# Two more units by 32x32 squares in an attention and feed-forward kernel, with their loads on GpSimd's queue and single rooms refilled behind each transpose

## The chip, the cores and the metric

The kernel runs on one core of a Trainium2 chip. A core has five engines with a queue of instructions each: TensorE (PE in the profile, its weight loads PEld), VectorE (DVE), ScalarE (ACT), GpSimd (POOL) and SyncE (SP), which here only issues transfers. The metric is the time of one execution on the device in microseconds (us).

## What is computed

Two blocks, one after the other. The first is a gated linear recurrence over 768 tokens for each of 4 batches and 8 heads, with 48 values a head. Its output, 3072 rows of 384, goes through a SwiGLU feed-forward block with 1536 hidden values. The three weight matrices arrive as 64-bit floats and are converted on the chip.

```python
f = 1.0 / (1.0 + np.exp(-f_logit))
for t in range(S):
    state = f[:, :, t, :, None] * state + np.einsum('bhd,bhe->bhde', k[:, :, t], v[:, :, t])
    y[:, :, t] = np.einsum('bhd,bhde->bhe', q[:, :, t], state)
...
x = np.ascontiguousarray(attn_out.transpose(0, 2, 1, 3)).reshape(B * S, H * D)
g = x @ w_gate
silu = g * (1.0 / (1.0 + np.exp(-g)))
val = x @ w_val
return (silu * val @ w_out).astype(np.float32)
```

## The kernel before

The work runs in `short_path`. The 768 tokens are cut into six chunks of 128. One *unit* of attention is one batch of one chunk, so units 0 to 3 are chunk 0, units 4 to 7 chunk 1, and so on to unit 23. A chunk that has gone through attention goes through the feed-forward block while the next chunk's attention is threaded between its matmuls. Chunk 0 uses plain products (`mlp_plain`, lines 790 and 813); chunks 1 to 5 use a scheme with fewer products (`mlp_fifteen`, line 992, and `down_seven`, lines 1091 and 1154), which needs sums of weights and of tokens on VectorE (lines 893 and 896).

`attention(u)` is a generator of 15 steps. In order: the gate's sigmoid and its transpose; the transpose of k; a running product of the gates backwards (line 605, `tail`, with a reciprocal at 608); k times tail (`kT`, line 559); for most later units a write of kT to memory, to be read back turned (lines 620 to 623 and 662); a running sum of products forwards (line 631, `gate`); the transpose of q; q times gate (`qT`, line 559, then a memset of one column of the gates by GpSimd at line 639); the scores on TensorE (line 651); their mask on VectorE (line 666); the decayed state; the output y (lines 687 to 727); and the new state (lines 732 to 741). The smallest product of a unit is kept in `least` (line 629 or 658), which at the end decides whether a general path has to redo everything.

The inputs lie token by token, and the attention wants them value by value, so f, k and q have to be transposed. There are two ways:

- Chunks 0 and 1 (`c < SQUARES`, `SQUARES = 2`): each input is loaded whole into a `raw` tile (line 444, on SyncE's queue), and TensorE transposes it in four blocks of 128x128 into PSUM (`transposed`, line 579), where ScalarE applies the sigmoid (line 590) and VectorE reads k and q in its multiplies. There are two raw tiles for each of f, k and q, used in turn. The rows are padded from 48 to 64 values; the padding of f holds 60, that of k and q holds 0 (line 343).
- Chunks 2 to 5: four transfers for each input (line 440, SyncE's queue) lay it into a `room` in a form whose 32x32 squares VectorE can transpose at once (line 593 for f, after a sigmoid in place at 584; line 601 for k; line 635 for q). `kp` is then the unit's qT tile and `qp` its tail tile, as rooms to transpose into. There is one room for each of f, k and q. They are made by `make_rooms` once the tiles of the early part are given up.

`load(u, what)` issues a unit's loads; `load_after(u)` issues those of a later one: for units 4 and 5 the loads of the unit two later, right after qT, and from chunk 2 on f, q and k of the next unit, all together after the transpose of q at line 635. The values v have tiles of their own.

What sets the order: the beginning, to line 1259, and everything from line 1286 on run in the order written, engine by engine (`in_order`). The latter part is written by a plan: a list of due times in units of a product's length (`times`, `CHAINS`, `SCORES`). Between the two, where units 4 to 7 are threaded through the plain feed-forward block (`attention_steps`, `take_turns`), each engine's order is chosen when the program is built, by what a model of the machine finds ready and by the order written. `attention_steps` cuts the 15 steps of a unit into four pieces of 3, 6, 3 and 3 and interleaves the pieces of neighbouring units. Conversions of weights (line 478 to 491) and weight sums are threaded through the same stretch; `behind` ties sums behind the last VectorE instruction written.

[...] a transfer on SyncE's queue that waits for a room holds all transfers behind it.

Of the kernel before, what the change touches and what calls it, by code (L numbers as in the profile page):

```python
# [9 lines left out]
FP32 = mybir.dt.float32  # L10
# [280 lines left out]
def short_path(ctx, tc, ident, least, judge, q, k, v, f_logit, moe_w_gate, moe_w_val, moe_w_out, out):  # L291
# [9 lines left out]
    nc = tc.nc  # L301
    B, H, S, D = q.shape
    C = 128
    NCH = S // C
    HP = H // 2
    W = 64
# [6 lines left out]
    NRAW = 2  # L313
    NROT = 2
    NV = 4
    SQUARES = 2
# [9 lines left out]
    first_pool = early.enter_context(tc.tile_pool(name="first", bufs=1))  # L326
# [9 lines left out]
                            pattern=[[1, C]], channel_multiplier=-1)  # L336


    raw = {nm: [first_pool.tile([128, H, W], FP32, tag=f"{nm}raw{i}", name=f"{nm}raw{i}") for i in range(NRAW)]
           for nm in "qkf"}  # L340
    for nm in "fkq":
        for t in raw[nm]:
            nc.gpsimd.memset(t[:, :, D:W], 60.0 if nm == "f" else 0.0)
# [20 lines left out]
    def pairs(t, off=0):  # L364
        return t[:, off:off + HP * N1].rearrange("p (a t) -> p a t", t=N1)
# [23 lines left out]
    units = [(b, c) for c in range(NCH) for b in range(B)]  # L389
# [5 lines left out]
    Q = 32  # L395
    NI = C // Q
    RUN = NI * D

    rooms = {}

    def make_rooms(pool):
        for nm in "fkq":
# [3 lines left out]
    def v_of(u):  # L406
        return vs[u % (NV if units[u][1] < SQUARES else NV // 2)]

    def squares(nm):
        return rooms[nm][:, Q:Q + HP * RUN].rearrange("t (a i e) -> t a i e", a=HP, i=NI)[:, :, :, 0:Q]  # L410

    def split_squares(nm):
        return squares(nm).rearrange("t a (j i) e -> t a j i e", j=2)

    def in_turn(t):

        return t.rearrange("p a (t i) -> p a i t", i=NI)

    def parted(t):

        return t.rearrange("p (j a t i) -> p a j i t", j=2, a=HP, i=NI // 2)

    def load(u, what="fkqv"):
        b, c = units[u]
        rows = slice(c * C, (c + 1) * C)
        inputs = dict(f=f_logit, k=k, q=q, v=v)
        for nm in "fkqv" if c < SQUARES else "fqkv":
            src = inputs[nm]  # L430
            if nm not in what:
                continue
            if nm == "v":
                dst = v_of(u)
            elif c < SQUARES:
                dst = raw[nm][u % NRAW]
            else:
                for n in range(4):
                    at = Q * (1 - n % 2)
                    nc.sync.dma_start(  # L440
                        out=rooms[nm][Q * n:Q * (n + 1), at:at + HP * RUN].rearrange("t (a e) -> t a e", a=HP),
                        in_=src[b, n // 2::2, rows, :].rearrange("a (t i) d -> t a (i d)", i=NI))
                continue
            nc.sync.dma_start(out=dst[:, :, 0:D], in_=src[b, :, rows, :].rearrange("h t d -> t h d"))

# [87 lines left out]
    def bank(name):  # L533
        return banks[-1].tile([128, 512], FP32, tag="a", name=name)
# [10 lines left out]
    def attention(u):  # L545
        b, c = units[u]
# [2 lines left out]
        gate, tail = (x[u % NROT if c < SQUARES else 0] for x in (gates, tails))  # L549

        diagonal = None

        def multiply(out, x, by):

            if c >= SQUARES:
                for_each = "p a (t j i) -> p a t j i"
                out, by = (t.rearrange(for_each, j=2, i=NI // 2) for t in (out, by))
                x = x.rearrange("p (j a t i) -> p a t j i", j=2, a=HP, i=NI // 2)
            nc.vector.tensor_tensor(out, x, by, ALU.mult)  # L559
# [16 lines left out]
        def transposed(name, src):  # L576
            p = bank(name)
            for a in range(HP):
                nc.tensor.transpose(p[:, a * C:(a + 1) * C],
                                    src[:, 2 * a:2 * a + 2, :].rearrange("t r d -> t (r d)"), ident)  # L580
            return p.rearrange("p (a t) -> p a t", t=C)

        if c >= SQUARES:
            nc.scalar.activation(squares("f"), squares("f"), AF.Sigmoid)
            if b == (c > SQUARES):

                nc.scalar.activation(spare, spare, AF.Silu)
        else:
            p = transposed("fTp", fr)
            nc.scalar.activation(pairs(gate)[:, :, 1:N1], p, AF.Copy if u in ahead else AF.Sigmoid)  # L590
        yield
        if c >= SQUARES:
            nc.vector.transpose(in_turn(pairs(gate)[:, :, 1:N1]), squares("f"))
        yield

        kT = att.tile([128, HP, C], FP32, tag="kT", name="kT")
        qT = att.tile([128, HP, C], FP32, tag="qT", name="qT", bufs=2)
        kp, qp = kT, qT
        if c >= SQUARES:
            kp = qT.rearrange("p a t -> p (a t)")  # L600
            nc.vector.transpose(parted(kp), split_squares("k"))
        yield

        n = HP * N1
# [2 lines left out]
        whole = pairs(tail)[:, :, 1:2]  # L607
        nc.vector.reciprocal(pairs(start)[:, :, 0:1], whole)
        yield
        if c < SQUARES:  # L610
            kp = transposed("kTp", kr)
            qp = transposed("qTp", qr)
        multiply(kT, kp, pairs(tail, 2)[:, :, 0:C])
        yield
        turned = SQUARES < c < NCH - 1
        if turned:


            beside = rooms["k"][:, 0:HP * C].rearrange("p (i m) -> p i m", i=NI)
            nc.vector.transpose(beside.rearrange("p i (a e) -> p a i e", e=Q), kT.rearrange("p a (i e) -> p a i e", e=Q))  # L620
            turn = turn_pool.tile([Q, NI, HP, NI, Q], FP32, tag="turn", name="turn")
            for r in range(NI):
                nc.sync.dma_start(out=turn[:, :, :, r, :].rearrange("t i a e -> t (i a) e"),
                                  in_=beside[Q * r:Q * (r + 1)].rearrange("t i (a e) -> t (i a) e", e=Q))
        yield

        if c >= SQUARES:

            nc.scalar.copy(least[:, u, :], whole.rearrange("p a t -> p (a t)"))
            whole = least[:, u, :].unsqueeze(2)  # L630
        nc.vector.tensor_tensor_scan(gate[:, 0:n], gate[:, 0:n], start, 1.0, op0=ALU.mult, op1=ALU.add)
        yield
        if c >= SQUARES:
            qp = tail[:, 0:HP * C]
            nc.vector.transpose(parted(qp), split_squares("q"))
            load_after(u)
        yield
        multiply(qT, qp, pairs(gate)[:, :, 1:N1])
        nc.gpsimd.memset(pairs(gate)[:, :, 0:1], 0.0)  # L639
        if 0 < c < SQUARES:  # L640
            load_after(u)
        if c < SQUARES:
            decay()
        yield
# [7 lines left out]
        if c < NCH - 1 and not turned:  # L652
            p = bank("kt")
            for a in range(HP):
                nc.tensor.transpose(p[:, a * C:(a + 1) * C], kT[:, a, :], ident)
        yield
        if c < SQUARES:
            nc.scalar.copy(least[:, u, :], whole.rearrange("p a t -> p (a t)"))
        if c < NCH - 1:
            kt = att.tile([128, HP * C], FP32, tag="kt", name="kt")  # L660
# [14 lines left out]
        if c and b < B - 1:  # L675
# [20 lines left out]
            for h in range(H):  # L696
                a, par = h // 2, h % 2
                f = h * D
                while f < (h + 1) * D:
                    n = min((h + 1) * D, (f // 128 + 1) * 128) - f  # L700
# [4 lines left out]
        else:  # L705
# [15 lines left out]
            for par in range(2):  # L721
                for n in range(DM // Q):
                    h = n // per * 2 + par
# [5 lines left out]
        if c < NCH - 1:  # L729
            p = bank("dS")  # L730
# [4 lines left out]
        if c >= SQUARES and u + 2 < len(units):  # L735
            load(u + 2, "v")
# [4 lines left out]
            nc.vector.tensor_tensor(states[b], decayed[:, :, 0:D], dS, ALU.add)  # L741
        yield

    def load_after(u):

        w = u + (1 if units[u][1] >= SQUARES else 2)
        if w < len(units) and (units[w][1] >= SQUARES) == (w == u + 1):
            load(w, "fkqv" if units[w][1] < SQUARES or w == SQUARES * B else "fkq")

    def attention_steps(c):  # L750

        runs = [attention(c * B + b) for b in range(B)]
        parts = [3, 6, 3, 3]
        order = sorted((2 * b + s, b, n) for b in range(B) for s, n in enumerate(parts))
        return [lambda b=b, n=n: [next(runs[b]) for _ in range(n)] for _, b, n in order]

    traced = nc.cur_bb.bb.instructions

    def in_order(since, engines):

# [6 lines left out]
    def keep_order(mine):  # L767
        for a, b in zip(mine, mine[1:]):
            tc.add_manual_dep(b, a.name, mybir.DependencyInfo(mybir.DependencyClass.NoSync,
                                                              mybir.DependencyReason.DATA), reason="order")  # L770
# [427 lines left out]
    for u in range(NRAW):  # L1198
        load(u, "fkq")
    load(0, "v")  # L1200
    mark = traced[-1]
    keep_warm(5)
    first = [attention(b) for b in range(B)]
    done = [0] * B

# [37 lines left out]

    hidden, last = mlp_plain(0)
    steps = attention_steps(1)
    sigmoid_ahead(B)
    joins.pop(0)()
# [41 lines left out]
    for c in range(2, NCH):  # L1289
        for b in range(B):  # L1290
            run = attention(c * B + b)
            waiting += [((c - 2) * whole + t, lambda run=run: next(run)) for t in times(c)[b]]
# [33 lines left out]
def kernel(  # L1326
# [22 lines left out]
    def judge(bank):  # L1349
# [13 lines left out]
        yield  # L1363

    short_path(tc, ident, least, judge, *args)
    with tc.If(redo[0] > 0, label="redo"):
        general_path(tc, *args)
# [32 lines left out]
```

## Time and profile before

| | us |
|---|---|
| median of 3 runs (607.35 to 608.85) | 607.47 |
| the profiled execution, its own time | 607.02 |
| its span, first to last instruction | 605.3 |

The stages of the profiled execution, from its timeline: attention of chunk 0 to 29.6; plain feed-forward of chunk 0 with attention of chunk 1 to 144.1; then the five chunks of the scheme with fewer products, to 600. The table shows the busy time of the engines in stretches, in us.

| stretch | length | TensorE | VectorE | ScalarE | GpSimd |
|---|---|---|---|---|---|
| 0 to 30 | 30 | 24.04 | 26.30 | 12.45 | 3.16 |
| 30 to 145 | 115 | 114.73 | 95.40 | 56.27 | 1.00 |
| 145 to 240 | 95 | 94.06 | 83.03 | 48.52 | 15.64 |
| 240 to 264 | 24 | 23.24 | 21.40 | 13.66 | 3.27 |
| 264 to 596 | 332 | 332.00 | 248.13 | 161.55 | 47.30 |

The clock granted to TensorE is full through all of it (0.998 in the mean). A matmul's recorded length overlaps that of the next, so what a group of matmuls holds the engine for is read from the start of one group to the start of the next.

### The profile page before, as it was taken

What the parts mean: (1) busy time and instruction counts of PE and PEld (TensorE: products, weight loads), DVE (VectorE), ACT (ScalarE), POOL (GpSimd) and SP (SyncE); (2) the same over time, 40 slices, a digit from 0 to 9 for tenths busy, and PEclk for the clock granted to TensorE, in tenths of its full rate; (3) what the DMA queues carried; (4) which work ended last, traced back from release to release, by engine and by line L of the source; (5) the groups of instructions that cost most, each with busy time, mean ns of one, the idle gap of its engine ahead of it and who ended that gap; (6) DMA issues with size and microseconds to landing.
All of it is one profiled execution on the core that took longest, in us unless ns stands there. A gap on an engine that the chain in (4) does not pass through costs nothing.

```text
span 605.3 us, 10815 instructions
## 1 busy us (share of the span) xinstructions
PE 592.4 (98%) x4028; PEld 487.7 (81%) x4028; DVE 476.5 (79%) x825; ACT 292.5 (48%) x557; POOL 70.4 (12%) x175
## 2 busy tenths in 40 slices
PE   7899999999999999999999999999999999999996
PEld 5744545667888899878899988899988899988896
DVE  7999895968999977989995978995878982566741
ACT  3567662314876521476632376742276740366600
POOL 1000000000030050030330030330030321000000
PEclk9999999999999999999999999999999999999999
DMA  9999371014231144443345243244231100100001
GB/s 198 242 251 357 136 198 27 7 27 138 80 82 48 45 117 104 104 112 96 73 112 127 78 117 95 53 120 110 74 105 52 28 7 9 53 1 1 1 1 56
DMA packets 110299, 55.11 MB, mean 91 GB/s; under 512 B 72992, under 2 KB 102688, under 8 KB 110240
## 3 DMA queue, kind: packets, MB, share of 16 engines
q1 hardware_dynamic: 103872, 47.67, 30.0%
q0 software_dynamic: 4352, 3.94, 1.9%
q10 hardware_dynamic: 2016, 2.75, 1.2%
q8 instruction: 33, 0.54, 0.4%
q14 instruction: 26, 0.21, 0.1%
HBM read 44.56 MB, written 6.82 MB: 85 GB/s over the span
## 4 chain that ended last, share of the span: by engine, by line
PE 87%; DVE 9%; issue 1%; ACT 1%; DMA 1%; SPq 0%; DVEq 0%; ACTq 0%
PE o L1091 19%; PE A L992 15%; PE B L992 12%; PE gate L790 5%; PE val L790 5%; PE c L992 5%; PE o L992 5%; PE sc L651 4%; PE o L1154 3%; PE o L813 3%; PE y L691 2%; PE y L712 2%; PE dS L732 2%; PE y L687 1%; DVE c L896 1%
## 5 line engine op out<-in xcount | busy, mean ns | idle before, releaser
L702 POOL DMA_DIRECT2D xT<-yT x120 | 60.1, 509 | 54.2 <-ACT yT L695 51.7
L992 PE MATMUL A<-xs,w_both 128*128 128x256 f32 x240 | 62.3, 382 | 0.8 <-ACT c L997 0.8
L1091 PE MATMUL o<-w_out,h 128*128 128x192 f32 x360 | 62.0, 327 | 0.5 <-DVE h L944 0.5
L1091 PEld LDWEIGHTS o<-w_out,h 128*128 128x128 f32 x360 | 58.7, 190 | 1.7 <-DVE h L944 0.8
L997 ACT COPY c<-A 128x512 f32<-128x512 f32 x40 | 23.3, 584 | 57.7 <-PE A L992 57.7
L997 ACT COPY aside<-A 128x512 f32<-128x512 f32 x60 | 35.1, 585 | 33.1 <-PE A L992 33.0
L992 PEld LDWEIGHTS A<-xs,w_both 128*128 128x128 f32 x240 | 44.8, 190 | 7.7 <-ACT c L997 1.2
L893 DVE TENSOR_TENSOR c<-c,aside 128x512 f32<-128x512 f32 x60 | 41.1, 685 | 12.4 <-ACT aside L997 10.8
L944 DVE TENSOR_TENSOR h<-h,c 128x256 f32<-128x256 f32 x100 | 40.5, 413 | 7.8 <-ACT h L1008 7.6
L666 DVE TENSOR_TENSOR A<-sc,causal 128x512 f32<-128x512 f32 x48 | 30.9, 684 | 17.6 <-PE sc L651 17.6
L1008 ACT ACTIVATE h<-c 128x256 f32<-128x256 f32 x100 | 39.2, 416 | 7.8 <-DVE c L893 5.6
L896 DVE TENSOR_TENSOR c<-c,aside 128x512 f32<-128x512 f32 x60 | 40.9, 682 | 2.5 <-ACT aside L997 2.5
L1091 PE MATMUL o<-ws,h 128*128 128x192 f32 x240 | 41.5, 328 | 0.2 <-DVE A L666 0.2
L992 PE MATMUL B<-xs,w_both 128*128 128x256 f32 x160 | 41.3, 380 | 0.1
L992 PE MATMUL A<-xs,extra 128*128 128x256 f32 x160 | 41.3, 380 | 0.0
L992 PE MATMUL c<-xT,w_both 128*128 128x256 f32 x160 | 41.2, 380 | 0.1
L992 PE MATMUL B<-xT,extra 128*128 128x256 f32 x160 | 41.1, 379 | 0.0
L639 POOL MEMSET gates<- 128x4 f32 x24 | 3.0, 123 | 326.3 <-DVE qT L559 321.2
L997 ACT COPY aside<-B 128x512 f32<-128x512 f32 x60 | 35.1, 586 | 9.6 <-PE B L992 7.0
L1091 PEld LDWEIGHTS o<-ws,h 128*128 128x128 f32 x240 | 39.1, 190 | 0.8 <-DVE A L666 0.4
L893 DVE TENSOR_TENSOR c<-c,o 128x384 f32<-128x384 f32 x15 | 8.3, 552 | 36.0 <-PE o L1091 36.0
L896 DVE TENSOR_TENSOR c<-o,c 128x512 f32<-128x512 f32 x40 | 27.3, 684 | 10.6 <-ACT h L1008 6.2
(142 smaller groups left out, 1199.2 us busy)
## 6 DMA issues: line engine op xcount, KB each, us to landing
fsquares<-in_f_logit_dram SPq DMA_DIRECT2D x64, 96.0 KB, 2.5
qsquares<-in_q_dram SPq DMA_DIRECT2D x64, 96.0 KB, 2.2
ksquares<-in_k_dram SPq DMA_DIRECT2D x64, 96.0 KB, 2.2
v<-in_v_dram SPq DMA_DIRECT2D x24, 192.0 KB, 2.8
w<-in_moe_w_gate_dram SPq DMA_DIRECT2D x6, 768.0 KB, 6.3
w<-in_moe_w_val_dram SPq DMA_DIRECT2D x6, 768.0 KB, 6.0
w<-in_moe_w_out_dram SPq DMA_DIRECT2D x6, 768.0 KB, 5.0
out_dram<-ob ACTq DMA_DIRECT2D x14, 192.0 KB, 2.5
```

The lines of the kernel that those rows point to most:

```text
L651: nc.tensor.matmul(sc[par][:, a * C:(a + 1) * C], lhsT=kT[r, a, :], rhs=qT[r, a, :], start=True, stop=True)
L666: nc.vector.tensor_tensor(A[:, par], sc[par].rearrange("p (a t) -> p a t", t=C), causal.unsqueeze(1).broadcast_to((128, HP, C)), ALU.mult)
L702: (nc.gpsimd if c >= SQUARES else nc.sync).dma_start(out=xT[c][f % 128:f % 128 + n, f // 128, b * C:(b + 1) * C], in_=yT[r:r + n, par, a / ...
L790: nc.tensor.matmul(p, lhsT=w[:, j, i, :], rhs=xT[c][:, i, :], start=(i == 0), stop=(i == KT - 1))
L813: nc.tensor.matmul(p, lhsT=hidden_tile(h, n // 2)[:, n % 2 * 2 + b // 2, b % 2 * C:(b % 2 + 1) * C], rhs=w_out[:, j, :], start=(n == 0), s ...
L893: nc.vector.tensor_tensor(dst, a, b, ALU.add)
L896: nc.vector.tensor_tensor(dst, a, b, ALU.subtract)
L944: lagging.append(lambda: f(*args))
L992: nc.tensor.matmul(p[name][:, n, :], lhsT=weights_of[a][:, n, j, :], rhs=tokens[b], start=fresh and n == 0, stop=True, skip_group_check=True)
L997: nc.scalar.copy(t, p[name])
L1008: nc.scalar.activation(dst, src[:, 0, :], AF.Silu)
L1091: nc.tensor.matmul(p[:, n, :], lhsT=lhsTs[j][:, n * C:(n + 1) * C], rhs=rhs[:, j, :], start=first and j == order[0] and n == 0, stop=j == ...
```

## The change

1. The raw tiles of f, k and q become one tile with two halves each (`both_raw`), and an early set of `rooms` is laid over both halves of each. No memset of the room's last columns is made for the early rooms.
2. `by_squares(u)` is true for unit 6 and later. Units 6 and 7 so leave the path over TensorE: sigmoid in place, three VectorE transposes, the multiplies on their results, and `least` copied ahead of the transpose of q.
3. Their f, k and q loads, twelve transfers a unit, are issued from GpSimd's queue, in an order tied by `keep_order`; v stays on SyncE's. Unit 6 is loaded right behind unit 5's transposes of k and q (the order is f, v, k, q).
4. `load_after` takes the inputs to load. From unit 6 on, the next unit's f is loaded behind the transpose of f, its k behind the transpose of k (where kT is turned through memory: behind that, since it uses k's room), its q behind the transpose of q. So unit 7's and all later units' loads are spread over the steps. Unit 8 is loaded as before.
5. Units 6 and 7 are cut into pieces of 1, 8, 3 and 3 steps.

```diff
-    raw = {nm: [first_pool.tile([128, H, W], FP32, tag=f"{nm}raw{i}", name=f"{nm}raw{i}") for i in range(NRAW)]
-           for nm in "qkf"}
+    both_raw = {nm: first_pool.tile([128, NRAW, H, W], FP32, tag=f"{nm}raw", name=f"{nm}raw") for nm in "qkf"}
+    raw = {nm: [both_raw[nm][:, i] for i in range(NRAW)] for nm in "qkf"}
...
-    rooms = {}
+    rooms = {nm: t.rearrange("p n h w -> p (n h w)")[:, 0:Q + HP * RUN] for nm, t in both_raw.items()}
+
+    def by_squares(u):
+        return u >= SQUARES * B - 2
...
-        for nm in "fkqv" if c < SQUARES else "fqkv":
+        for nm in "fqkv" if c >= SQUARES else "fvkq" if by_squares(u) else "fkqv":
...
-            elif c < SQUARES:
+            elif not by_squares(u):
                 dst = raw[nm][u % NRAW]
             else:
+                since = len(traced)
                 for n in range(4):
                     at = Q * (1 - n % 2)
-                    nc.sync.dma_start(
+                    (nc.sync if c >= SQUARES else nc.gpsimd).dma_start(
...
+                if c < SQUARES:
+                    by_pool.extend(ins for ins in traced[since:] if ins.engine == mybir.EngineType.Pool)
+                    keep_order(by_pool[-5:])
                 continue
...
-        if c >= SQUARES:
+        if in_squares:
             nc.vector.transpose(in_turn(pairs(gate)[:, :, 1:N1]), squares("f"))
-        yield
-
+            load_after(u, "f")
+        yield
+
+        turned = SQUARES < c < NCH - 1
...
-        if c >= SQUARES:
+        if in_squares:
             kp = qT.rearrange("p a t -> p (a t)")
             nc.vector.transpose(parted(kp), split_squares("k"))
+            if not turned:
+                load_after(u, "k")
...
-        if c < SQUARES:
+        if not in_squares:
             kp = transposed("kTp", kr)
             qp = transposed("qTp", qr)
+            if by_squares(u + 1):
+                load(u + 1)
...
+            load_after(u, "k")
...
             nc.vector.transpose(parted(qp), split_squares("q"))
-            load_after(u)
+            load_after(u, "qv" if c < SQUARES else "q")
         yield
         multiply(qT, qp, pairs(gate)[:, :, 1:N1])
         nc.gpsimd.memset(pairs(gate)[:, :, 0:1], 0.0)
-        if 0 < c < SQUARES:
-            load_after(u)
...
-    def load_after(u):
-
-        w = u + (1 if units[u][1] >= SQUARES else 2)
-        if w < len(units) and (units[w][1] >= SQUARES) == (w == u + 1):
-            load(w, "fkqv" if units[w][1] < SQUARES or w == SQUARES * B else "fkq")
+    def load_after(u, what):
+
+        if u + 1 < len(units) and u + 1 != SQUARES * B:
+            load(u + 1, what)
...
-        parts = [3, 6, 3, 3]
-        order = sorted((2 * b + s, b, n) for b in range(B) for s, n in enumerate(parts))
+        order = sorted((2 * b + s, b, n) for b in range(B)
+                       for s, n in enumerate((1, 8, 3, 3) if by_squares(c * B + b) else (3, 6, 3, 3)))
```

More of the change, by code (lines that the diff above doesn't have):

```diff
@@ L423, in parted @@
         return t.rearrange("p (j a t i) -> p a j i t", j=2, a=HP, i=NI // 2)
+    traced = nc.cur_bb.bb.instructions
+    by_pool = []
     def load(u, what="fkqv"):
@@ L551, in attention @@
         diagonal = None
+        in_squares = by_squares(u)
         def multiply(out, x, by):
-            if c >= SQUARES:
+            if in_squares:
                 for_each = "p a (t j i) -> p a t j i"
@@ L581, in transposed @@
             return p.rearrange("p (a t) -> p a t", t=C)
-        if c >= SQUARES:
+        if in_squares:
             nc.scalar.activation(squares("f"), squares("f"), AF.Sigmoid)
-            if b == (c > SQUARES):
+            if c >= SQUARES and b == (c > SQUARES):
                 nc.scalar.activation(spare, spare, AF.Silu)
@@ L591, in attention @@
         yield
-        if c >= SQUARES:
+        if in_squares:
             nc.vector.transpose(in_turn(pairs(gate)[:, :, 1:N1]), squares("f"))
+            load_after(u, "f")
         yield
+        turned = SQUARES < c < NCH - 1
         kT = att.tile([128, HP, C], FP32, tag="kT", name="kT")
@@ L598, in attention @@
         kp, qp = kT, qT
-        if c >= SQUARES:
+        if in_squares:
             kp = qT.rearrange("p a t -> p (a t)")
             nc.vector.transpose(parted(kp), split_squares("k"))
+            if not turned:
+                load_after(u, "k")
         yield
@@ L609, in attention @@
         yield
-        if c < SQUARES:
+        if not in_squares:
             kp = transposed("kTp", kr)
             qp = transposed("qTp", qr)
+            if by_squares(u + 1):
+                load(u + 1)
         multiply(kT, kp, pairs(tail, 2)[:, :, 0:C])
         yield
-        turned = SQUARES < c < NCH - 1
         if turned:
@@ L624, in attention @@
                                   in_=beside[Q * r:Q * (r + 1)].rearrange("t i (a e) -> t (i a) e", e=Q))
+            load_after(u, "k")
         yield
-        if c >= SQUARES:
+        if in_squares:
             nc.scalar.copy(least[:, u, :], whole.rearrange("p a t -> p (a t)"))
@@ L632, in attention @@
         yield
-        if c >= SQUARES:
+        if in_squares:
             qp = tail[:, 0:HP * C]
             nc.vector.transpose(parted(qp), split_squares("q"))
-            load_after(u)
+            load_after(u, "qv" if c < SQUARES else "q")
         yield
@@ L656, in attention @@
         yield
-        if c < SQUARES:
+        if not in_squares:
             nc.scalar.copy(least[:, u, :], whole.rearrange("p a t -> p (a t)"))
@@ L742, in attention @@
         yield
-    def load_after(u):
-        w = u + (1 if units[u][1] >= SQUARES else 2)
-        if w < len(units) and (units[w][1] >= SQUARES) == (w == u + 1):
-            load(w, "fkqv" if units[w][1] < SQUARES or w == SQUARES * B else "fkq")
+    def load_after(u, what):
+        if u + 1 < len(units) and u + 1 != SQUARES * B:
+            load(u + 1, what)
     def attention_steps(c):
         runs = [attention(c * B + b) for b in range(B)]
-        parts = [3, 6, 3, 3]
-        order = sorted((2 * b + s, b, n) for b in range(B) for s, n in enumerate(parts))
+        order = sorted((2 * b + s, b, n) for b in range(B)
+                       for s, n in enumerate((1, 8, 3, 3) if by_squares(c * B + b) else (3, 6, 3, 3)))
         return [lambda b=b, n=n: [next(runs[b]) for _ in range(n)] for _, b, n in order]
-    traced = nc.cur_bb.bb.instructions
     def in_order(since, engines):
```

## The prediction

> **What bounds the kernel now.** I read three things in order: the page's first part (who is busy), the TensorE timeline (where it stops, and at what spacing its work runs), then VectorE by stretches (what room it has for work moved to it). First, busy time over the span:
>
> ```profile
> PE 592.4 (98%) x4028; PEld 487.7 (81%) x4028; DVE 476.5 (79%) x825; ACT 292.5 (48%) x557; POOL 70.4 (12%) x175
> ```
>
> TensorE covers 592.4 of 605.3 us, and its waits for other engines after its first instruction are under 6 us, most of them in the first 30. So time comes off in two ways only: less TensorE work, or one of the few TensorE stops removed. The TensorE timeline around the last two units of chunk 1 (start, length, operation; the bracket is idle time before it and what ended it):
>
> ```profile
> 84.33 0.60 PE L579 MATMUL fTp<-idf,fraw 128*128 128x128 f32 x4
> 84.77 5.32 PE L790 MATMUL val<-xT,w_both 128*128 128x512 f32 x12
> ...
> 99.92 0.60 PE L579 MATMUL kTp<-idf,kraw 128*128 128x128 f32 x4
> 100.35 0.60 PE L579 MATMUL qTp<-idf,qraw 128*128 128x128 f32 x4
> 100.79 2.74 PE L790 MATMUL val<-xT,w_both 128*128 128x512 f32 x6
> ...
> 120.66 0.60 PE L579 MATMUL kTp<-idf,kraw 128*128 128x128 f32 x4
> 121.09 0.60 PE L579 MATMUL qTp<-idf,qraw 128*128 128x128 f32 x4
> 121.53 2.75 PE L813 MATMUL o<-w_out,h 128*128 128x384 f32 x8
> 124.55 1.16 PE L651 MATMUL sc<-qT,kT 48*128 48x128 f32 x16 [0.27 <-DVE qT L559]
> ```
>
> The reader should take spacings, not lengths: the lengths overlap, and four transposes hold TensorE for 84.77 - 84.33 = 0.44 us. From 30 us to 205 us TensorE stops once, at 124.55, for 0.27 us, and VectorE ends that stop. It stops again for 0.54 us at 205.97, 0.19 us at 223.03, and at 262.46, of which more below. VectorE is the engine that takes the moved work; its room by stretches (columns: stretch, sum of busy, then TensorE, its weight loads, VectorE, ScalarE, GpSimd, clock, DMA share, GB/s):
>
> ```profile
> 90.00:107.20 17.20, 17.20 (x106) 9.71 (x106) 8.39 (x14) 4.80 (x8) 0.11 (x1) 1.00 0.11 24
> 107.20:129.00 21.80, 21.53 (x134) 14.03 (x134) 21.66 (x35) 6.95 (x12) 0.11 (x1) 1.00 0.04 10
> 129.00:133.80 4.80, 4.80 (x81) 3.30 (x80) 0.01 (x2) 0.48 (x1) 0.00 (x0) 1.00 0.01 3
> ```
>
> VectorE is half idle from 90 to 107 (8.8 us free), full from 107 to 129, idle from 129 to 134. The full stretch is the danger.
>
> [...] the trace agrees (0.60 us lengths at 0.44 us spacing), so I price removed transposes by spacing. [...] The trace has the same loads from SyncE at a median of 2.5 us to landing, and small GpSimd-issued transfers (24 KB) at 2.5 us, so I take 2.5. [...]
>
> **The change part by part.**
>
> *TensorE, units 6 and 7.* Twenty-four transposes go. Unit 6: 0.44 (f) + 0.87 (k and q, 99.92 to 100.79). Unit 7: 0.43 (f, 110.21 to 110.64) + 0.87 (120.66 to 121.53). Sum 2.61 us, all on the engine that sets the end, at full clock.
>
> *VectorE, the same units.* It gains per unit one f transpose (1112 ns, the row of line 593), one of k (704 ns, line 601) and one of q (697 ns, line 635): 2.51 us a unit, 5.03 us in all. The two multiplies stay: from PSUM 678 and 688 ns, from SBUF 673 and 684 ns, no difference. Free time for it: 8.8 us before 107, 4.8 us after 129. Unit 6's chain ran at 91.5 to 102, for scores at 106.04, beside that idle time. The weight joins it might push back have room: the last gate-and-value join ends at 84.8 us and is used at 97.3.
>
> *Does unit 7's chain end in time?* The order outside the handwritten stretches is chosen by when work is ready. Today k and q of unit 7 wait for TensorE's transposes at 120.66, so kT and qT run at 123.1 to 124.4. Afterwards they need only loads and VectorE. Unit 7's f is fetched right behind unit 6's f transpose (about 91), so it lands near 96 (four issues of some 0.55 us, the 509 and 558 ns of GpSimd's rows, and 2.5 us). Its sigmoid, f and k transposes and first scan then fit the idle time before 107. kT can start once unit 6's own transposes have read the single kT tile (107.8 today). What remains, kT 0.68, q 0.70, qT 0.69, is 2.1 us in the 15 us before TensorE reaches unit 7's scores, at 124.28 - 2.61 = 121.67. I take no new stop, and leave the present 0.27 us out of the gain. Bounds: from -0.27 to +5.2 us, the latter worked out under the rivals.
>
> *ScalarE.* Sigmoid of a square is 631 ns against 597 from PSUM: 0.07 us in all. If unit 7's sigmoid comes among the Silus, one more pair of table loads, 2.6 us, on an engine busy 4.8 of 17.2 us there: nothing. The copy into `least` now stands ahead of the q transpose; ScalarE waits idle nearly 10 us there, but a copy queued behind one that waits for TensorE would hurt; that is inside the 5.2.
>
> *Queues.* SyncE loses six of its 192 KB loads and keeps both v loads; the weight fetches behind them can only come sooner. GpSimd gains 24 issues, 13 us at 0.55, on an engine busy 1.0 us from 30 to 145. Behind its waiting loads stands only the memset of a gate column, needed by the unit two later. [...] I price it at nothing, with up to 2 us as the worst.
>
> *Chunks 2 to 5.* The next f is asked for behind the f transpose instead of behind the q transpose, and k behind its last reader. Today SyncE asks late, and ScalarE, which works in order, waits with the copies that free TensorE's banks:
>
> ```profile
> 255.16 2.05 SPq L440 DMA_DIRECT2D fsquares<-in_f_logit_dram  x4
> ...
> 259.46 1.28 ACT L584 ACT_TABLE_LOAD   x1 [3.70 <-DMA fsquares<-in_f_logit_dram]
> ...
> 262.46 1.13 PE L992 MATMUL A<-xs,w_both 128*128 128x256 f32 x4 [0.76 <-ACT c L997]
> ```
>
> The f room was empty at 244.7 (transpose at 243.56, 1.10 us), so the load lands about 249 and the 0.76 us stop goes. ScalarE's other two long waits, 4.88 us before 240.16 and 5.16 us before 323.82, precede no TensorE stop: zero. What is late next is a bank or a VectorE sum, at most a few tenths. On SyncE the k load stands behind the four turn writes, which read its room: it holds the queue until they land (2.1 us), with the q and v loads and the read back of the turn behind it. q then has over 5 us left, and the turn's read needs that landing anyway: nothing.
>
> *Sum.* -2.61 - 0.76 = -3.37 us. On the profiled execution's own 607.02 us (span 605.3) that is 603.65. The median before is 607.47, 0.45 higher; I take 603.7.
>
> **The rivals.**
>
> 1. *Slower, by one mechanism: unit 7's added transposes stand in the full VectorE stretch, 107 to 129, ahead of its scores.* If the order keeps the chain where it is, qT ends at 124.40 + 2.51 = 126.9 while TensorE arrives at 121.67: a stop of 5.2 us, less what was removed, 5.24 - 3.37 = +1.87, so 608.9. It decides from qT later than 121.67 + 3.37 = 125.0, only 0.6 us later than now. For it: that stretch is 21.66 of 21.80 us busy and already makes TensorE's one stop. Against: the first scan of unit 7 ran at 113.64, ahead of work written before it, so the order does bring ready work forward; and other matmuls (48 more of line 813 come after these scores) can fill in.
>
> 2. *No change to speak of: VectorE becomes the bound later.* From 175 to 209 VectorE has almost no gap (14.93 and 14.48 of 15 us in 180 to 210). If it enters that stretch no sooner than now, TensorE's 2.61 us are waited away at 205, and 0.76 remains: 606.3. Against: at 175.36 VectorE waited 1.41 us for TensorE's scores, so an earlier TensorE moves it too.
>
> 3. *The early loads don't come early*, because SyncE or GpSimd is held by something in front: 0.76 lost, 604.4. It lies within the range of the forecast.
>
> **How the numbers follow.** Forecast with rival 3: 0.69, 601.8 to 605 (the low end adds smaller bank waits behind ScalarE and the stops at 124 and 205). Rival 2: 0.14, around 606.3. Rival 1: 0.17, around 608.9. The range, 601.8 to 606.8, leaves out rival 1 and little else. A measurement of this kernel tells from no change about 0.3%, 1.8 us, so faster means below 605.65: 0.69; same 0.14; slower 0.17.
>
> **What would show it.** Right: 24 fewer transposes of line 579; six more VectorE transposes before 135; unit 7's scores near 121.7 with no wait; the first product of chunk 1 at about 141.5 instead of 144.1; no stop near 259. Wrong: a TensorE stop before unit 7's scores ended by VectorE's qT; ScalarE waiting for squares loaded by GpSimd; a longer stop near 203.

## The result, and the profile after

Six executions of the changed kernel take 604.13 us in the median (603.96 to 605.36), six of the kernel before 607.42 (607.22 to 608.85): a ratio of 0.9943, 95% interval 0.993 to 0.9956. The forecast was 603.7 in a range of 601.8 to 606.8, "faster" at 0.69.

The first profile of the changed kernel happens to be of its longest execution (605.36). Its first part, to be read against the same line of before:

```profile
PE 591.9 (98%) x4004; PEld 487.6 (81%) x4004; DVE 480.3 (80%) x831; ACT 294.8 (49%) x559; POOL 86.2 (14%) x199
```

The counts answer to the edit: 24 TensorE instructions fewer, six VectorE instructions more, 24 on GpSimd more, and two more on ScalarE, which are table loads (32 where there were 30). Yet TensorE's busy time fell by 0.5 us only. A good part of what is missing lies in the clock of one stretch that the change doesn't touch, 28 to 32 us (columns: stretch, length, TensorE busy and its instructions, granted clock, DMA share, GB/s):

```profile
26.00:28.00 2.00, 1.36 (x24) 0.99 0.92 176
28.00:30.00 2.00, 2.00 (x40) 0.50 0.87 186
30.00:32.00 2.00, 2.00 (x17) 0.65 1.05 333
```

In that execution TensorE was granted 0.50 and 0.65 of its clock in the last two of these stretches and lost 1.36 us: the next transposes of f, at 32.29 before, start at 33.65. The changed kernel was therefore run and profiled once more, unaltered (`again`: 604.1, 603.87 to 604.33, six executions; ratio 0.994, 0.9928 to 0.9953). Its profiled execution took 603.87 with a span of 602.1, a full clock (1.00) and 590.9 us of TensorE busy time; the profile of before had a full clock (1.00) from 28 to 32 us too, so these two are compared from here on.

The TensorE timeline of `again`, at the places that the prediction spoke of:

```profile
104.73 1.16 PE L666 MATMUL sc<-qT,kT 48*128 48x128 f32 x16
105.83 0.66 PE L670 MATMUL kt<-idf,kT 128*128 128x128 f32 x4
106.32 5.33 PE L825 MATMUL o<-w_out,h 128*128 128x384 f32 x16
111.57 0.43 PE L702 MATMUL y<-qT,decayed 48*64 48x128 f32 x2
111.93 2.85 PE L825 MATMUL o<-w_out,h 128*128 128x384 f32 x8
114.71 0.66 PE L702 MATMUL y<-qT,decayed 48*64 48x128 f32 x14
...
122.13 1.16 PE L666 MATMUL sc<-qT,kT 48*128 48x128 f32 x16
...
131.26 10.59 PE L825 MATMUL o<-w_out,h 128*128 128x384 f32 x32
141.68 1.03 PE L1004 MATMUL A<-xs,w_both 128*128 128x256 f32 x4
...
203.55 1.57 PE L1103 MATMUL o<-w_out,h 128*128 128x192 f32 x8 [0.55 <-DVE h L956]
...
256.43 1.13 PE L1004 MATMUL A<-xs,w_both 128*128 128x256 f32 x4
```

The reader should see four things. Unit 6's scores (104.73) start 1.31 us earlier than before (106.04), the exact price of its twelve transposes. Unit 7's scores start at 122.13 with no wait, where they waited at 124.55. The first product of chunk 1 is at 141.68 instead of 144.10: 2.42 us came from this part. And the row at 256.43 has no bracket, where 262.46 of before had a 0.76 us stop. From that first product to the end of the span, before took 605.3 - 144.10 = 461.2 us and `again` 602.1 - 141.68 = 460.42: 0.78 us came from chunks 2 to 5. Together 3.20, the difference of the two spans.

### The profile page after: what moved, and what is told of

It is laid out like the page before. It is cut to its first block, busy times and chain, and to the rows that moved or that the text cites. A ratio compares the mean times of both kernels' runs of the same rounds, so it can differ in the third digit from the quotient of the medians.

```text
span 603.5 us, 10851 instructions
## 1 busy us (share of the span) xinstructions
PE 591.9 (98%) x4004; PEld 487.6 (81%) x4004; DVE 480.3 (80%) x831; ACT 294.8 (49%) x559; POOL 86.2 (14%) x199
## 4 chain that ended last, share of the span: by engine, by line
PE 93%; DVE 5%; issue 1%; ACT 0%; DVEq 0%; ACTq 0%
PE o L1103 19%; PE A L1004 16%; PE B L1004 13%; PE c L1004 5%; PE o L1004 5%; PE gate L802 5%; PE o L825 5%; PE val L802 5%; PE sc L666 4%; PE o L1166 3%; PE y L706 3%; PE y L727 2%; PE dS L747 2%; PE y L702 2%; PE kt L670 1%; DVE c L908 1%
```

## The experiments

### The two parts of the change, each alone

`only_squares` keeps the squares of units 6 and 7 and their queue, but from chunk 2 on loads f, q and k of the next unit together, as before:

```diff
-            load_after(u, "f")
+            if c < SQUARES:
+                load_after(u, "f")
...
-            load_after(u, "qv" if c < SQUARES else "q")
+            load_after(u, "qv" if c < SQUARES else "fqk")
```

> Units 6 and 7 by squares from GpSimd's queue, but from chunk 2 on f, q and k loaded together behind the transpose of q, as before. By the sum of the prediction: -2.61 us against the kernel before (ratio 0.9957), the first product of chunk 1 at about 141.5, and the stop of 0.76 us for the bank behind the late f is there again near 259.5. If the placement of the loads carries most of the gain: ratio above 0.998. If VectorE takes the saved TensorE time back at the end of the first product stretch: a stop of 2 us or more near 203.

`only_loads` is the kernel before, with the loads of chunks 2 to 5 spread as in the change and nothing else:

```diff
             nc.vector.transpose(in_turn(pairs(gate)[:, :, 1:N1]), squares("f"))
+            load_after(u, "f")
...
-            load_after(u)
+            load_after(u, "q")
```

> Units 6 and 7 over TensorE as before; only the loads of chunks 2 to 5 stand each behind the transpose that empties the room. By the sum of the prediction: -0.76 us (ratio 0.9987), no stop at 262, the rest of the TensorE timeline unchanged. If these loads come no earlier: ratio 1.000 and the stop still there. If they free more than the one stop, in bank waits too short to be told as idle: ratio below 0.998.

And the changed kernel once more:

> The changed kernel once more, for a second profile: in the first one TensorE ran at a clock of 0.80 from 25 to 30 us and was 1.36 us late from there on, before anything that the change touches. If that was of this one execution: span 602.4, clock 1.00 in 25 to 30, first product of chunk 1 at 141.5 to 141.9, ratio to the kernel before 0.9945. If the slow clock comes from the change: again 0.80 there, and a span of 603.5.

Measured in one set, against 607.48 for the kernel before: `again` 604.1; `only_squares` 605.11 (604.58 to 606.12), ratio 0.9957 (0.9943 to 0.9971); `only_loads` 606.23 (605.63 to 607.27), ratio 0.9977 (0.9968 to 0.9987). The two parts are separate gains, of 2.4 and 1.3 us by the medians; their sum, 3.6, agrees with the 3.4 of both together within what these intervals allow. Of the first part's pieces only the queue was tried apart (below), not the new cut of the steps into 1, 8, 3 and 3. In the timeline of `only_squares` the stop of chunk 2 is back, at its new place:

```profile
261.07 1.13 PE L1004 MATMUL A<-xs,w_both 128*128 128x256 f32 x4 [0.49 <-ACT c L1009]
```

So that stop is due to the late loads. Its length differs between executions with late loads: 0.76 before, 0.49 here, 1.04 in `late_load` and 1.19 in `before_warm`, two runs told of below. How an earlier f removes it shows in the timeline of `again`, SyncE's and ScalarE's rows:

```profile
242.29 1.83 SPq L447 DMA_DIRECT2D fsquares<-in_f_logit_dram  x4
...
253.37 1.28 ACT L595 ACT_TABLE_LOAD   x1
254.66 0.63 ACT L595 ACTIVATE fsquares<-fsquares 128x512 f32<-128x512 f32 x1
...
257.60 0.59 ACT L1009 COPY c<-A 128x512 f32<-128x512 f32 x1 [1.77 <-PE A L1004]
```

f is asked for at 242.29 instead of 255.16. Before, ScalarE waited 3.70 us for it, with the copies behind it; now the table load starts without a wait, and ScalarE waits for TensorE's products, not they for it.

### Does the queue matter?

The prediction priced the choice of queue at nothing. `by_sync` is the changed kernel with the loads of units 6 and 7 on SyncE's queue:

```diff
-                    (nc.sync if c >= SQUARES else nc.gpsimd).dma_start(
+                    nc.sync.dma_start(
```

> The changed kernel with the loads of units 6 and 7 on SyncE's queue instead of GpSimd's. If the queue doesn't matter, since both have time to spare: within 0.1% of the changed kernel, ratio to before 0.994 to 0.9955. If SyncE's loads, waiting for rooms, hold the weight fetches behind them: joins of weights later than 84.8 us for gate and value, TensorE stops before 105 us, ratio 0.998 or above.

It takes 608.21 (606.4 to 609.53, 22 executions), ratio 1.0003 (0.9995 to 1.0012): the whole gain is gone. SyncE's queue, VectorE and TensorE in the timeline of `by_sync`:

```profile
93.38 6.21 SPq L714 DMA_DIRECT2D xT<-yT  x10
99.63 1.06 SPq L447 DMA_DIRECT2D qraw<-in_q_dram  x2
100.73 1.46 SPq L468 DMA_DIRECT2D w<-in_moe_w_out_dram  x3
...
105.77 0.61 DVE L497 TENSOR_SCALAR up<-w 128x768 uint16<-128x768 uint16 x1 [2.77 <-DMA w<-in_moe_w_out_dram]
...
114.72 4.34 PE L822 MATMUL o<-w_out,h 128*128 128x384 f32 x8 [3.09 <-DVE w_out L498]
```

Unit 7's q has to wait until unit 6's q has been transposed out of the room, at 88.44; its first two transfers go at 89.18. Next in the queue are ten transfers of unit 5's output (yT), from 93.38 to 99.6. The other half of q follows, and behind it three fetches of `w_out`, which start at 100.73; in `again` the last two go at 75.98. VectorE waits for that weight until 105.77. TensorE reaches it at 111.6 and waits 3.09 us for it to be joined. The release of TensorE's wait names VectorE; what was late first was a transfer, behind one that waited for a room. The expectation looked for this at the gate and value weights; it came at `w_out`. Then TensorE runs at a lower clock:

```profile
114.00:116.00 2.00, 1.27 (x4) 0.98 0.00 0
116.00:118.00 2.00, 2.00 (x4) 0.50 0.00 0
118.00:120.00 2.00, 2.00 (x22) 0.66 0.00 0
```

`sync_but_q7` moves only unit 7's q back to GpSimd:

```diff
-                    (nc.sync if c >= SQUARES else nc.gpsimd).dma_start(
+                    (nc.gpsimd if u == SQUARES * B - 1 and nm == "q" else nc.sync).dma_start(
```

> As the version with the loads on SyncE's queue, but unit 7's q alone on GpSimd's. On SyncE that load waited for unit 6's q transpose, the writes of yT behind it, and three weight fetches behind those, at 100.7 us instead of 76 to 81; TensorE then stopped 3.09 us at 114.7 for a weight join. If that one load is the cause: no such stop, ratio to before 0.994 to 0.9955. If all the waiting loads on SyncE hold the fetches: a stop again, ratio 0.998 or above.

605.76 (605.29 to 609.3), ratio 0.9981 (0.9967 to 0.9994). One of the six loads undoes a part of the loss: 2.4 of 4.1 us by the medians, about a third by the ratios, since five of the 13 executions are above 606.7. Fetches of `w_out` still go as late as 99.49. In the profiled execution (606.79) the stop at 114.7 is gone, and an earlier one stands in the timeline:

```profile
104.40 0.60 DVE L500 TENSOR_SCALAR up<-w 128x768 uint16<-128x768 uint16 x1 [4.13 <-DMA w<-in_moe_w_out_dram]
...
105.62 0.91 PE L825 MATMUL o<-w_out,h 128*128 128x384 f32 x2 [1.64 <-DVE h L816]
```

It has the same origin: VectorE waits 4.13 us for `w_out`, and the hidden values (h, line 816) that TensorE needs come right behind that, at 104.89.

### The rival that would have made it slower

Rival 1 said that unit 7's chain on VectorE might run in the full stretch ahead of its scores. `late_chain` makes it so: it ties unit 7's transpose of f, and with it all that follows, behind unit 6's new state.

```diff
             nc.vector.transpose(in_turn(pairs(gate)[:, :, 1:N1]), squares("f"))
+            if u == SQUARES * B - 1:
+                keep_order([state_of[u - 1], traced[-1]])
```

> The changed kernel with unit 7's f transpose tied behind unit 6's new state on VectorE, so that unit 7's whole VectorE chain starts near 117.5 us (of a profile in which unit 7's scores start at 122.1) instead of 93. By the slower rival of the prediction: the chain of 6.5 us with the sums between ends at 125 to 127, TensorE stops before the scores by 3 to 5 us, and the ratio to before is 0.999 to 1.003. If other matmuls fill in, since the order of this stretch is chosen by what is ready: no stop over 0.5 us, ratio below 0.9965.

606.94 (605.39 to 609.59, 22 executions), ratio 0.9984 (0.9973 to 0.9995), 2.8 us over `again`. In the timeline of `late_chain`:

```profile
114.07 0.67 PE L705 MATMUL y<-qT,decayed 48*64 48x128 f32 x16
...
118.42 1.09 DVE L605 STREAM_TRANSPOSE gates<-fraw 128x512 f32<-128x512 f32 x1
...
123.47 0.68 DVE L571 TENSOR_TENSOR qT<-tails,gates 128x512 f32<-128x512 f32 x1
124.21 1.91 PE L669 MATMUL sc<-qT,kT 48*128 48x128 f32 x16 [1.99 <-DVE qT L571]
...
132.01 0.86 PE L730 MATMUL y<-qT,diagonal 128*32 128x128 f32 x24
```

The stop is where the rival put it, before unit 7's scores and ended by qT, but 1.99 us long and not 5.2. From f's transpose to the end of qT it took 5.7 us, with no sums of weights in between. A second loss stood in no list: the matmuls behind the stop run slowly. From the scores to the y group TensorE needs 132.01 - 124.21 = 7.80 us here and 128.97 - 122.13 = 6.84 us in `again`, which has two more matmuls of the feed-forward block in between (0.33 us each, by the 5.25 us of the 16 at 106.32). That is 1.6 us lost besides the stop. (The y group starts only 3.04 us later than in `again`, because unit 6's y, at 114.07, stays in one group here. In `again` it is split, at a price worked out below.) The clock by stretches:

```profile
122.00:124.00 2.00, 0.22 (x1) 1.00 0.09 25
124.00:126.00 2.00, 1.79 (x16) 0.61 0.00 0
126.00:128.00 2.00, 2.00 (x8) 0.54 0.00 0
128.00:130.00 2.00, 2.00 (x8) 1.00 0.00 0
```

The 22 times lie in two groups, ten from 605.4 to 605.9 and nine from 606.9 to 607.6, with three above. The granted clock, recorded as a mean over each execution, separates them: 0.997 to 0.999 in the lower group, 0.995 or 0.996 in the upper, 0.990 to 0.993 in the three above. The middles of the two groups lie 1.6 us apart, as much as was lost besides the stop. So the lower group is most likely the stop without the loss of clock; only one execution, of the upper group, was profiled.

### One more unit, and the spread

If removed transposes are worth their spacing as long as VectorE has room, unit 5 should give its 1.31 us as well. `three_units`:

```diff
-        return u >= SQUARES * B - 2
+        return u >= SQUARES * B - 3
...
-    load(B + 1)
+    if not by_squares(B + 1):
+        load(B + 1)
```

> The changed kernel with unit 5 by squares as well, twelve more transposes off TensorE, 1.31 us by spacing. If VectorE has room between 40 and 75 us: 602.8, ratio to before 0.9925. If VectorE, full there with weight joins (29.08 of 30 us from 30 to 60 in the changed kernel), passes its added 2.5 us on to TensorE, or unit 5's loads come too late: no gain over the changed kernel, ratio 0.994 to 0.997, with a TensorE stop for a join or for unit 5's qT.

602.97 (602.39 to 603.83), ratio 0.9925 (0.991 to 0.9941): below the kernel before, and all six executions below the fastest of the changed kernel's twelve (603.87). Its rows in the TensorE timeline have no waits before the scores:

```profile
103.45 1.16 PE L666 MATMUL sc<-qT,kT 48*128 48x128 f32 x16
...
120.85 1.16 PE L666 MATMUL sc<-qT,kT 48*128 48x128 f32 x16
...
140.40 1.03 PE L1004 MATMUL A<-xs,w_both 128*128 128x256 f32 x4
```

Unit 6's and 7's scores and the first product (141.68 in `again`) all come 1.28 us earlier. VectorE is then busy 29.18 of 30 us from 30 to 60 and 29.16 from 60 to 90. But it was busy 29.08 and 29.00 there in `again` too, and unit 5 still gave its full 1.3 us, so this share doesn't tell whether a fourth unit would gain; that was not tried.

Executions of one kernel lie 2 us and more apart (606.88 to 609.17 for the kernel before, in one set of 32). Two ideas on that were tried, and neither narrowed the times. `late_load` took the kernel before and asked for unit 6's loads later, so that four weight fetches went ahead of them:

```diff
+            if u == B + 1:
+                load(u + 1)
...
-        if 0 < c < SQUARES:
+        if 0 < c < SQUARES and u > B:
```

> The kernel before with one edit: unit 6's raw loads are asked for at unit 5's transposes of k and q instead of behind unit 4's qT, so that on SyncE's queue four weight fetches stand ahead of them. If those loads at 37 to 42 us held back the fetches, and with them the VectorE joins in front of unit 5's scores near 78 us: median 606.9 instead of 607.5 (ratio 0.999), lowest time as before, and the spread of the runs falls from some 2 us to under 1. If the weight fetches don't matter: ratio 1.000 and the same spread.

607.61 (607.22 to 608.88) against 607.41, ratio 0.9999 (0.999 to 1.0008), and no narrower. `before_warm` and `three_warm` put two matmuls on a scratch tile into each of TensorE's three short stops between 20 and 28 us, which the clock of 0.50 had followed in the first profile after:

```diff
+        if u in (B - 2, B - 1):
+            keep_warm(2)
...
+            if u == B - 1:
+                keep_warm(2)
```

> The kernel before with a few matmuls on a scratch tile put ahead of the scores of units 2 and 3 and ahead of unit 3's y, so that TensorE has work in the short stops there. Theory that a half clock near 28 us, following those stops, makes the spread between executions of one kernel: no execution above 608.0 where 11 of 42 of the kernel before were, median 607.0 to 607.2, ratio 0.999. Rival, the spread has another origin: the same share of executions above 608, median 607.4, ratio 1.000, and in the profile the clock from 28 to 32 us is either as before.

> The kernel with squares for three units, with the same matmuls on a scratch tile. If a half clock near 28 us makes its spread: 602.4 to 602.6, its executions within 0.6 us, ratio 0.9915 to 0.9925. If the added matmuls delay other work instead: 603.4 or more. If they do neither: as three_units, 602.97 with a spread of 1.4.

`before_warm` takes 607.41 (607.02 to 609.0), ratio 0.9998 (0.9989 to 1.0006), with two of 13 executions above 608 against three of 17 of the kernel before beside it; `three_warm` takes 603.29 (602.42 to 604.26), ratio 0.9924 (0.991 to 0.9938), like `three_units`. The profiled execution of `before_warm` was its longest, 609.0, and had a full clock (1.00) from 28 to 32 us. What it had instead is in its timeline:

```profile
76.41 0.56 DVE L488 TENSOR_SCALAR top<-top 128x768 int32<-128x768 int32 x1
77.01 0.96 DVE L491 CUSTOM_DVE_ANT_0 w_out<-top,up 128x1536 uint16<-128x1536 uint16 x1
77.88 0.68 DVE L559 TENSOR_TENSOR kT<-kTp,tails 128x512 f32<-128x512 f32 x1
78.48 0.68 DVE L559 TENSOR_TENSOR qT<-qTp,gates 128x512 f32<-128x512 f32 x1
79.31 1.16 PE L653 MATMUL sc<-qT,kT 48*128 48x128 f32 x16 [1.45 <-DVE qT L559]
```

Unit 5's kT came at 77.88, where the profile of before has it at 75.63, behind conversions of weights that came later; their fetches went out some 1.8 us later (42.40 against 40.64). `only_loads`' profiled execution had the same stop, 1.20 us at 78.87. So at least two events make the spread, a lost clock and weights that arrive late; why they come in some executions and not in others stays open. The mean clocks of the executions say the same. Of 91 executions of the kernel before, in three sets, 24 took more than 608 us; 14 of these, and no other, had a clock of 0.996 or less. Of the 13 of `before_warm` none was below 0.998, the two slow ones included. That the scratch matmuls made this difference isn't shown: at 14 in 91, a run of 13 without one comes by chance about once in nine times.

## Why the prediction held, step by step

- *TensorE, -2.61 and the 0.27 stop left out.* The 24 transposes went, at the spacing that was read, and the stop went too: 2.88 in full. 2.42 came, 0.46 less, all of it ahead of unit 7's scores, which were forecast at 121.67 and came at 122.13. From those scores to the first product both kernels take 19.55 us. Of the 0.46, 0.36 is the step from 111.57 to 111.93: two matmuls of unit 6's y run ahead, and the other 14 at 114.71 take 0.59 up to the next group, as the whole 16 did before (0.60). The 40 matmuls of line 825 in between hold TensorE for 13.38 us instead of 13.29. The prediction summed what is removed and didn't ask what the new order splits. That 2.42 lies so near 2.61 is partly luck: the stop that it left out made up for more than half of the split that it missed.
- *VectorE, +5.03 us at nothing.* Right. In the 17.2 us from 90 to 107.2 it is busy 12.26 us where it was 8.39. Unit 7's f, k and q are through at 112.9, nine microseconds before its scores:

```profile
93.23 1.09 DVE L604 STREAM_TRANSPOSE gates<-fraw 128x512 f32<-128x512 f32 x1
...
107.73 0.68 DVE L570 TENSOR_TENSOR kT<-qT,tails 128x512 f32<-128x512 f32 x1
...
108.93 0.70 DVE L652 STREAM_TRANSPOSE tails<-qraw 128x512 f32<-128x512 f32 x1
...
112.20 0.68 DVE L570 TENSOR_TENSOR qT<-tails,gates 128x512 f32<-128x512 f32 x1
```

  These rows of `again` are the chain that the prediction worked out (kT from 107.8 on, f's transpose in the idle time before 107). The whole-run busy time rose by 3.6 us, less than the sum of the six lengths. In part this is because neighbouring records overlap on VectorE too (the first row above lasts 1.09 us, and the next operation starts 0.95 us after it); the rest is not explained.
- *ScalarE.* One more pair of table loads came, as allowed for, and cost nothing. It waits once for a square loaded by GpSimd, 0.57 us up to 67.19 in the first profile, and no TensorE stop follows; in `again` it doesn't.
- *Queues at nothing.* Right for the kernel as changed, and the weakest of the reasons. The text looked at what GpSimd's queue would suffer and said of SyncE only that fetches behind the removed loads "can only come sooner". It did not ask what those loads would have done on SyncE. `by_sync` gives that: 608.21 - 604.1 = 4.1 us by the medians, the whole gain. The choice of queue is a condition of the gain, not a detail. The worst case of 2 us for GpSimd's queue was the author's estimate; no run shows it.
- *Landing and issue.* Unit 7's f, predicted to land near 96, is already transposed at 93.23: unit 6's f was transposed at 69.1, not about 91, and unit 7's was asked for at 77.88. GpSimd's 24 issues cost 16.0 us busy (86.4 against 70.4), 0.67 each and not 0.55; its f loads took a median of 6.3 us from issue to landing, not 2.5. In `again` no engine stood waiting for a load from GpSimd.
- *Chunks 2 to 5, -0.76.* 0.78 between the two profiles. By medians `only_loads` alone gives 1.3, with an interval (0.8 to 1.9 us, from its ratio of 0.9968 to 0.9987) that begins where the forecast lies. The other profiles narrow this. From the first product of chunk 1 to the end of the span the four with late loads take 461.2 to 461.5 us, the eight with spread loads 460.1 to 460.7: about 0.95 us between their means, and 0.5 to 1.4 between single executions. The mechanism was right and the price a little low; the stop that it was read from was 0.49 to 1.19 us long in other executions.
- *Rivals.* 1 is a real mechanism, whose condition did not hold; the stop was priced too high (5.2 us against the 1.99 of `late_chain`), and the clock loss behind a stop (1.6) was missing. 2 would have shown as a longer stop at VectorE's full stretch: it is 0.55 at 203.55, 0.54 at 205.97 before. 3 did not happen.
- *The baseline.* The sum of -3.37 is almost what the medians give, 604.1 - 607.48 = -3.38. The forecast took it off the profiled execution, which was 0.45 us faster than the median, and added only 0.05 back. With all of the 0.45 it would have been 604.1.

## What to carry to other kernels

Price work removed from the bounding engine at its spacing (0.44 us for four transposes here, where their records last 0.60), and keep a few tenths for groups that a new order splits (0.36 here). When a load has to wait for a room to be emptied, ask what stands behind it in its queue: on SyncE's queue the six loads cost all that the change gains (4.1 us by `by_sync`), and a third to over half of that came from one of them. In `late_chain` a stop of TensorE of 1.99 us cost 1.6 us besides its length, at a clock of 0.61 and 0.54 behind it; so look at the clock of the stretch after a stop.

## What the hardware showed that was not expected

- After stops of 1.64, 1.99 and 3.09 us TensorE's granted clock fell. In stretches of 2 us it was 0.80, 0.50 and 0.85 after the first (106 to 112 us in `sync_but_q7`), 0.61 and 0.54 after the second (124 to 128 us in `late_chain`), 0.98, 0.50 and 0.66 after the third (114 to 120 us in `by_sync`). What is missing from full clock adds up to 1.7 us each time, and in `late_chain` it cost 1.6 us. After stops of 1.20 us (`only_loads`), 1.34 (`three_warm`, at 91.90) and 1.45 (`before_warm`) the clock stayed at 1.00, and after one of 1.62 us too (at 10.04 in `three_units`, whose clock is 1.00 from 0 to 30 us), so the length alone doesn't seem to decide. After three short stops (0.36, 0.79 and 0.65 us in `again`) the clock from 28 to 30 us was 0.50 in the first profile of the changed kernel and in those of `only_squares` and `late_load`, and 1.00 in those of before, `again` and `three_units`. What decides it was not shown.
- GpSimd's transfers differ by when they are made. From the list of transfers of `again` (queue, count, KB each, median us from issue to landing) and its timeline:

```profile
fraw<-in_f_logit_dram POOLq DMA_DIRECT2D x8, 96.0 KB, 6.3
kraw<-in_k_dram POOLq DMA_DIRECT2D x8, 96.0 KB, 2.5
qraw<-in_q_dram POOLq DMA_DIRECT2D x8, 96.0 KB, 2.9
```

```profile
56.70 4.90 POOL L447 DMA_DIRECT2D fraw<-in_f_logit_dram  x4 [10.83 <-PE fTp L590]
72.27 2.25 POOL L447 DMA_DIRECT2D kraw<-in_k_dram  x4 [10.68 <-PE kTp L590]
```

  Four issues take 4.90 us at 57 and 2.25 at 72, with the same sizes. In the first profile of the changed kernel they take 4.58 us at 58.05 and 2.18 at 73.62. VectorE's busy share doesn't tell the two places apart there: 4.60 of 4.60 us from 58.0 to 62.6 and 2.18 of 2.20 from 73.6 to 75.8. The DMA engines are fuller at the first (share 0.65 against 0.40), but unit 7's f, at 78.44, takes 2.20 us at a share of 0.98 (78.4 to 80.6), and in `by_sync` SyncE issues the transfers of unit 6's f in 1.76 us at 56.46. So full DMA engines alone don't make the issues slow; what does was not shown.
